# Three weight-splitting steps moved behind a pair's second addition, and one pair's x and convolution moved behind the gates, in a fused soft-cap attention and gated-convolution kernel

## The chip, the core and the metric

The kernel runs on one core of one Trainium2 chip. Such a core has four compute engines that run their own instruction streams in order and meet at semaphores: TensorE (PE, matmuls; its weight loads are shown as PEld), VectorE (DVE), ScalarE (ACT) and GpSimd (POOL); SyncE (SP) issues the DMAs here. The metric is the time of one execution in microseconds (us).

## The reference

Soft-capped attention over 8 batches, 12 heads, 448 positions and head size 64, then a gated causal convolution and two projections over 768 channels:

```
scores = cap * tanh(q @ k.T / sqrt(64) / cap)
attn   = softmax(scores);  x = attn @ v            # heads side by side: x is (8, 448, 768)
gate   = sigmoid(sum over k<5 of conv_w[k] * x shifted by k rows)
out    = (gate * (x @ w_val)) @ w_out              # weights are float64 in memory
```

## The kernel before

**Pairs.** Two heads make a pair, six pairs a batch, 48 pairs p in all (pair p belongs to batch p // 6). For each pair q and k are loaded in 32-column blocks and turned on DVE (L291); four key chunks i of 112 rows give scores on PE (`pss`, L312), tanh and exp on ACT (L320, L324, tile `pt`), the product with v on PE (`psa`, L349), and the row sums on PE (`psz`, L361). To save PE work DVE first adds exponentials of chunks: `add` i=0 for chunks 0 and 1, i=1 ("the second addition") for chunks 2 and 3 (both L334, tile `pa`), and from pair 11 on a third one that joins the two (L331). Pairs 7 to 10 feed both sums to PE, so that `psz` has one matmul couple on the first sum and one on the second. DVE then turns the sums (L369, `zt`), forms reciprocals (L375, L376), spreads them (L382) and multiplies (L390) into `u`, the transposed x of the pair.

**x and the convolution.** ACT rounds `u` to `xh` (L395), DVE takes the rest `xl` (L226), and the five taps build the pre-gate: the first on ACT (L407) up to pair 10 and on DVE (L409) from pair 11, the others on DVE (L411).

**Projections.** When a batch's six x are there, one `val` per 128 columns accumulates 18 matmuls in a `psf` bank (L432 to L434), ACT takes the sigmoids (L417), DVE multiplies (L438, "gate"), ACT rounds to `g_h` (L441), DVE takes the rest `g_l` (L226), and `out_part` multiplies with `wo` (L461 to L463) into a `psf` bank that ACT copies to `osb` (L469) for the store. There are two `psf` banks.

**Weights.** `w_val` and `w_out` are split into two float32 parts in twelve steps n = 0 to 11, called W0 to W11 here. A step has a `first` on ACT (L126, L127), a `second` on DVE (L130, L131) and a `third` on DVE (L134 to L136). W0 to W5 make `wv`, W6 to W8 the first half of the columns of `wo`, W9 to W11 the second half. Raw tiles are single: W n's raw load (L258) is issued when W n-1's `second` has read its tile.

**Order.** Nothing is scheduled automatically: each step gets a due time in units of pairs, from tables (`PAIRED` for pairs 7 to 10, `STEADY` for 11 and 12, `SPLIT` after) or lists, and the sorted list is the order on every engine. Pair p's second addition is due at p + 1.03, W n's `first` at `W_AT[n]`, its `second` 0.02 and its `third` 0.05 later. `LATE_X` puts a pair's `xl` at p + 1.76 and its taps at p + 1.78 to 1.89 in place of 1.58 and 1.60 to 1.70; the loop gives it to the first pair of a batch (p % 6 == 0). Gates of batch b with due times from 6b + 7.62 on are multiplied in the pairs after the batch's last.

Of the kernel before, what the change touches and what calls it, by code (L numbers as in the profile page):

```python
# [86 lines left out]
NEARLY, NPAIRED, NPLAIN = 6, 11, 13  # L87
# [6 lines left out]
OUT_LATE = (9.80, 10.36, 10.74, 11.74, 12.36, 12.60)  # L94
PART = 0.13
KEEP_AT = 10.2
W_AT = (0.70, 1.70, 2.70, 3.70, 4.70, 5.70, 7.1, 8.0, 8.9, 9.7, 10.4, 11.0)
W_LOAD = -0.5
W_SECOND, W_THIRD, W_THIRD_EARLY = 0.02, 0.05, 0.71
W_FREE = 11.3  # L100
# [87 lines left out]
def fast_path(tc, io, u2, q, k, v, w_val, conv_w, w_out, out, capt):  # L188
# [9 lines left out]
    NP = B * NPAIR  # L198
# [12 lines left out]
    with ExitStack() as ctx:  # L211
# [264 lines left out]
        cw_steps = []  # L476
        events = []
        tables = [EARLY if p < NEARLY else SIXTH if p == NEARLY else PAIRED if p < NPAIRED else STEADY if p < NPLAIN else SPLIT for p in range(NP)]
        for p in range(NPLAIN, NP):
            if p % NPAIR == 0:  # L480
                tables[p] = tables[p] | LATE_X

        def at(when, f, *a):
            events.append((when, len(events), f, a))
# [19 lines left out]
        for b in range(B):  # L504
# [15 lines left out]
            for m, y in enumerate(OUT_ODD if b % 2 else OUT_LATE if b == B - 2 else OUT_EVEN):  # L520
# [3 lines left out]
                at(t0 + y + 0.40, store_out, b, m)  # L524
        for n, t0 in enumerate(W_AT):
            third = [x + (W_THIRD if x > NEARLY else W_THIRD_EARLY) for x in W_AT]
            at(W_AT[n - 1] + W_SECOND if n else W_LOAD, weight_load, n)
            at(third[n - 1] if n else W_LOAD, late_load, n)
# [135 lines left out]
def kernel(tc, q, k, v, cap, w_val, conv_w, w_out, out):  # L664
    nc = tc.nc
    with tc.tile_pool(name="cap_pool", bufs=1) as pool, tc.tile_pool(name="io", bufs=2) as io:
        capt = pool.tile([P, 1], F32, name="capt")
        nc.sync.dma_start(capt, cap.rearrange("(o c) -> o c", o=1).partition_broadcast(P))

        pad = conv_w.shape[0] - 1  # L670
        u2 = [pool.tile([P, pad + q.shape[2]], F32, name=f"u{i}") for i in range(2)]
        for t, src in zip(u2, (q, k)):
            load_blocks(nc, t[:, pad:], src, 0)
        mag = pool.tile([1, 1], F32, name="mag")
        nc.vector.scalar_tensor_tensor(mag, capt[0:1], -1.0, capt[0:1], ALU.mult, ALU.max)
        small = pool.tile([1, 1], I32, name="small")
        nc.vector.tensor_scalar(small, mag, CAP_FAST, None, ALU.is_le)
        flag = nc.values_load(small, min_val=0, max_val=1)
        with tc.If(flag != 0) as cmp:
            fast_path(tc, io, u2, q, k, v, w_val, conv_w, w_out, out, capt)  # L680
        with cmp.Else():
            general_path(tc, q, k, v, w_val, conv_w, w_out, out, capt)
# [30 lines left out]
```

## Time and profile before

| | |
|---|---|
| median of three runs | 754.6 us (752.79 to 754.98) |
| the profiled execution | 752.42 us |
| its span, first to last instruction | 750.7 us |
| PE busy | 725.2 us, 97% of the span |
| DVE busy | 592.8 us, 79% |
| ACT busy | 538.1 us, 72% |
| mean granted TensorE clock | 0.997 |

The profiled execution lies 2.2 us below the median, and 1.7 us of it lie outside the span. Durations below are from this execution. The trace lists instructions by start time, with the length of one or of a merged run, and in square brackets how long the engine sat idle just before and which instruction ended that. Merged runs overlap the next instruction by the pipeline's depth: three matmuls of one line 0.2 us apart each show 0.36 us.

### The profile page before, as it was taken

The page shows a single profiled execution, that of the slowest core. Times are in us where ns is not written, and L with a number is a line of the kernel's source. Part 1 is how long each engine was busy: PE and PEld are TensorE (multiplying, and loading weights), DVE is VectorE, ACT ScalarE, POOL GpSimd, SP SyncE. Part 2 cuts the span into 40 slices and gives each one's busy share as a digit, 9 for nine tenths or more (in the row PEclk, how much of TensorE's full clock was granted, in tenths as well). Part 3 has the DMA queues.
Part 4 walks back from the last instruction along what each step waited for, and adds up shares of the span by engine and source line. Part 5 has one row for each costly group of instructions (what it writes and reads, how often), then busy time and mean ns, then how long its engine had stood idle before and what let it go on. Part 6 is the DMA issues. An engine that isn't in the chain of part 4 may idle for free.

```text
span 750.7 us, 10859 instructions
## 1 busy us (share of the span) xinstructions
PE 725.2 (97%) x3972; PEld 487.0 (65%) x3972; DVE 592.8 (79%) x972; ACT 538.1 (72%) x708; POOL 7.5 (1%) x16
## 2 busy tenths in 40 slices
PE   5999998999899999999999999999999999999997
PEld 2333654557667777577677767767766776675997
DVE  2799988888987689888898769988898778997410
ACT  4899967777777687777957678686976669775311
POOL 0000000000000000000000000000000000000000
PEclk9999999999999999999999999999999999999999
DMA  6998866754223332234232333223322333210001
GB/s 111 225 214 193 221 162 147 198 122 77 44 38 80 80 74 38 49 81 83 48 61 49 80 71 68 44 68 73 72 38 60 82 77 53 50 34 22 22 21 67
DMA packets 241820, 63.75 MB, mean 85 GB/s; under 512 B 228448, under 2 KB 235616, under 8 KB 241760
## 3 DMA queue, kind: packets, MB, share of 16 engines
q1 hardware_dynamic: 241760, 62.98, 38.0%
q8 instruction: 33, 0.54, 0.3%
q14 instruction: 27, 0.22, 0.1%
HBM read 51.94 MB, written 11.01 MB: 84 GB/s over the span
## 4 chain that ended last, share of the span: by engine, by line
PE 44%; DVE 24%; ACT 24%; issue 5%; SPq 2%; DMA 1%; DVEq 0%; ACTq 0%
ACT pt L320 7%; PE psf L461 7%; PE pss L312 7%; ACT pt L324 6%; PE psf L463 6%; PE psf L462 6%; PE psa L349 6%; DVE pa L334 5%; DVE gate L411 3%; ACT gate L417 3%; PE psf L432 3%; PE psz L361 2%; PE psf L434 2%; PE psf L433 2%; DVE g_l L226 2%
## 5 line engine op out<-in xcount | busy, mean ns | idle before, releaser
L320 ACT ACTIVATE pt<-pss,rc 112x896 f32<-112x896 f32 x192 | 185.8, 1004 | 29.0 <-PE pss L312 29.0
L324 ACT ACTIVATE pt<-pt,capt 112x896 f32<-112x896 f32 x192 | 189.3, 1039 | 0.1
L349 PE MATMUL psa<-pt,vn 112*64 112x448 f32 x720 | 147.7, 546 | 0.0
L411 DVE SCALAR_TENSOR_TENSOR gate<-u,cw,gate 128x448 f32<-128x448 f32 x192 | 132.4, 689 | 5.8
L461 PE MATMUL psf<-wo,g_h 128*128 128x384 f32 x336 | 116.9, 348 | 0.0
L463 PE MATMUL psf<-wo,g_l 128*128 128x384 f32 x336 | 112.7, 335 | 0.0
L462 PE MATMUL psf<-wo,g_h 128*128 128x384 f32 x336 | 112.5, 335 | 0.0
L432 PE MATMUL psf<-xh,wv 128*128 128x448 f32 x288 | 108.9, 378 | 2.1 <-DVE gate L438 2.0
L434 PE MATMUL psf<-xl,wv 128*128 128x448 f32 x288 | 104.4, 362 | 0.0
L433 PE MATMUL psf<-xh,wv 128*128 128x448 f32 x288 | 104.3, 362 | 0.0
L334 DVE TENSOR_TENSOR pa<-pt 112x896 f32<-112x896 f32 x84 | 91.1, 1084 | 12.6 <-ACT pt L324 12.6
L349 PEld LDWEIGHTS psa<-pt,vn 112*64 112x64 f32 x720 | 47.7, 136 | 81.2 <-issue 69.8
L395 ACT CAST xh<-u 128x448 fp32r<-128x448 f32 x48 | 27.1, 565 | 76.8 <-DVE u L390 76.7
L461 PEld LDWEIGHTS psf<-wo,g_h 128*128 128x128 f32 x336 | 63.0, 188 | 22.6 <-issue 18.3
L369 DVE STREAM_TRANSPOSE zt<-psz 128x448 f32<-128x448 f32 x45 | 28.9, 642 | 57.1 <-PE psz L361 57.0
L432 PEld LDWEIGHTS psf<-xh,wv 128*128 128x128 f32 x288 | 54.0, 187 | 28.0 <-issue 18.3
L441 ACT CAST g_h<-gate 128x448 fp32r<-128x448 f32 x48 | 26.3, 563 | 51.9 <-DVE gate L438 51.8
L463 PEld LDWEIGHTS psf<-wo,g_l 128*128 128x128 f32 x336 | 63.1, 188 | 0.3
L462 PEld LDWEIGHTS psf<-wo,g_h 128*128 128x128 f32 x336 | 63.1, 188 | 0.0
L312 PE MATMUL pss<-qt,kt 64*112 64x448 f32 x208 | 50.6, 606 | 9.6 <-DVE guard L235 7.8
L469 ACT COPY osb<-psf 128x384 f32<-128x384 f32 x56 | 26.8, 479 | 44.3 <-PE psf L463 44.3
L312 PE MATMUL pss<-qh,kh 64*112 64x448 f32 x280 | 58.5, 412 | 0.0
(74 smaller groups left out, 906.4 us busy)
## 6 DMA issues: line engine op xcount, KB each, us to landing
vn<-in_v_dram SPq DMA_DIRECT2D x96, 112.0 KB, 2.6
out_dram<-osb SPq DMA_DIRECT2D x56, 192.0 KB, 1.9
qn<-in_q_dram SPq DMA_DIRECT2D x188, 56.0 KB, 2.5
kn<-in_k_dram SPq DMA_DIRECT2D x188, 56.0 KB, 2.4
w_raw<-in_moe_w_val_dram SPq DMA_DIRECT2D x12, 384.0 KB, 4.5
w_late<-in_moe_w_val_dram SPq DMA_DIRECT2D x12, 384.0 KB, 4.3
w_raw<-in_moe_w_out_dram SPq DMA_DIRECT2D x12, 384.0 KB, 3.7
w_late<-in_moe_w_out_dram SPq DMA_DIRECT2D x12, 384.0 KB, 4.6
```

What stands on the lines that cost most here:

```text
L312: nc.tensor.matmul(ps[:CH, j, :S], st[x][r, c], st[y][r], start=(n == 0), stop=(n == len(parts) - 1))
L320: nc.scalar.activation(st["p", i], st.pop(("s", i)), AF.Tanh, scale=rc8[:CH])
L324: nc.scalar.activation(t, t, AF.Exp, scale=capt[:CH])
L334: nc.vector.tensor_tensor(st["a", i], st["p", 2 * i], st["p", 2 * i + 1], op=ALU.add)
L349: nc.tensor.matmul(st["o"][r, :S], vloads[p][:, j, i], t[:, j], start=(i == 0), stop=(i == NKT - 1))
L411: nc.vector.scalar_tensor_tensor(g, u[:, i:i + S], cw[:, hp, i:i + 1], g, ALU.mult, ALU.add)
L432: nc.tensor.matmul(o, w_h, xh, start=(c == 0), stop=False)
L433: nc.tensor.matmul(o, w_l, xh, start=False, stop=False)
L434: nc.tensor.matmul(o, w_h, xl, start=False, stop=(c == NCC - 1))
L461: nc.tensor.matmul(o, g_h[:, d, s], w_h, start=(d == 0), stop=False)
L462: nc.tensor.matmul(o, g_h[:, d, s], w_l, start=False, stop=False)
L463: nc.tensor.matmul(o, g_l[:, d, s], w_h, start=False, stop=(d == NCC - 1))
```

## The change

Three entries of `W_AT` are raised and the loop that gives out `LATE_X` starts at pair 11 in place of 13, which adds pair 12 (the first pair of the third batch, due when the second batch's gates are).

```diff
-W_AT = (0.70, 1.70, 2.70, 3.70, 4.70, 5.70, 7.1, 8.0, 8.9, 9.7, 10.4, 11.0)
+W_AT = (0.70, 1.70, 2.70, 3.70, 4.70, 5.70, 7.1, 8.035, 9.035, 9.7, 10.4, 11.035)
...
-        for p in range(NPLAIN, NP):
+        for p in range(NPAIRED, NP):
             if p % NPAIR == 0:
                 tables[p] = tables[p] | LATE_X
```

**W8 on DVE** (near 117 to 124 us of the trace). `pa_1086` before and `pa_1072` after are the same tile, the second addition of pair 8; the first five rows before are W8's. Before:

```order
L226 TENSOR_TENSOR g_l<-gate,g_h 128x448
L130 TENSOR_SCALAR w_t<-w_t 128x768
L131 TENSOR_TENSOR wo<-w_t,w_raw 128x2x384
L134 TENSOR_SCALAR w_late<-w_late 128x2x384
L135 TENSOR_SCALAR w_t<-wo 128x768
L136 SCALAR_TENSOR_TENSOR wo<-w_late,w_t 128x2x384
L438 TENSOR_TENSOR gate<-psf,gate 128x448
L334 TENSOR_TENSOR pa_1086<-pt 112x896
L226 TENSOR_TENSOR g_l<-gate,g_h 128x448
```

After, on the same engine at the same place:

```order
L226 TENSOR_TENSOR g_l<-gate,g_h 128x448
L438 TENSOR_TENSOR gate<-psf,gate 128x448
L334 TENSOR_TENSOR pa_1072<-pt 112x896
L226 TENSOR_TENSOR g_l<-gate,g_h 128x448
L130 TENSOR_SCALAR w_t<-w_t 128x768
L131 TENSOR_TENSOR wo<-w_t,w_raw 128x2x384
L134 TENSOR_SCALAR w_late<-w_late 128x2x384
L135 TENSOR_SCALAR w_t<-wo 128x768
L136 SCALAR_TENSOR_TENSOR wo<-w_late,w_t 128x2x384
```

All five W8 steps stand behind a gate product, the second addition and a `g_l`; on ACT, W8's L126 and L127 stand behind the rounding `g_h` (L441) of that gate in place of ahead of it. W7 and W11 move by less: only their L130 and L131 stood ahead of the second addition (of pairs 7 and 10), and stand right behind it now, with L134 to L136 as before; ACT's order does not change there.

**Pair 12 on DVE** (near 187 to 196 us). `u_63` is pair 12's x. Before, from the `kl` of the next pair on:

```order
L226 TENSOR_TENSOR kl<-kt,kh 128x448
L226 TENSOR_TENSOR xl<-u_63,xh 128x448
L409 TENSOR_SCALAR gate<-u_63,cw 128x448
L411 SCALAR_TENSOR_TENSOR gate<-u_63,cw,gate 128x448
L438 TENSOR_TENSOR gate<-psf,gate 128x448 x2
L411 SCALAR_TENSOR_TENSOR gate<-u_63,cw,gate 128x448 x3
L226 TENSOR_TENSOR g_l<-gate,g_h 128x448 x2
L438 TENSOR_TENSOR gate<-psf,gate 128x448
L334 TENSOR_TENSOR pa_1745<-pt 112x896
```

After:

```order
L226 TENSOR_TENSOR kl<-kt,kh 128x448
L438 TENSOR_TENSOR gate<-psf,gate 128x448 x2
L226 TENSOR_TENSOR g_l<-gate,g_h 128x448 x2
L226 TENSOR_TENSOR xl<-u_63,xh 128x448
L409 TENSOR_SCALAR gate<-u_63,cw 128x448
L411 SCALAR_TENSOR_TENSOR gate<-u_63,cw,gate 128x448 x4
L438 TENSOR_TENSOR gate<-psf,gate 128x448
L334 TENSOR_TENSOR pa_1745<-pt 112x896
```

Two gate products and their two `g_l` stand ahead of pair 12's six steps, which still stand ahead of the third gate product and the second addition of pair 13. The instructions of PE, POOL and SP stand in the same order in both kernels; a weight's raw load on SP still waits for the `second` of the weight before it.

## Rows read from the trace of the kernel before

**Rows 1.** The page's chain that ended last, shares of the span by engine.

```profile
PE 44%; DVE 24%; ACT 24%; issue 5%; SPq 2%; DMA 1%; DVEq 0%; ACTq 0%
```

**Rows 2.** Waits of PE, 80 to 220 us: total, times, longest.

```profile
PE psz L361 <- DVE pa L334: 4.1, 3, 2.3
```

**Rows 3.** Timeline around W7 (start, length, engine, line), 99 to 108 us.

```profile
100.40 1.96 ACT L324 ACTIVATE pt<-pt,capt 112x896 f32<-112x896 f32 x2
...
103.20 0.56 DVE L130 TENSOR_SCALAR w_t<-w_t 128x768 int32<-128x768 int32 x1 [1.11 <-ACT w_t L126]
...
105.05 1.09 DVE L334 TENSOR_TENSOR pa<-pt 112x896 f32<-112x896 f32 x1
...
106.06 0.58 DVE L134 TENSOR_SCALAR w_late<-w_late 128x768 int32<-128x768 int32 x1
...
106.19 0.97 PE L361 MATMUL psz<-pa,ones 112*64 112x448 f32 x4 [0.65 <-DVE pa L334]
```

**Rows 4.** Timelines of DVE, ACT and PE around W8, 116 to 144 us.

```profile
118.98 0.56 DVE L130 TENSOR_SCALAR w_t<-w_t 128x768 int32<-128x768 int32 x1 [1.65 <-ACT w_t L126]
119.95 0.96 DVE L131 TENSOR_TENSOR wo<-w_t,w_raw 128x768 fp32r<-128x768 f32 x1 [0.41 <-ACT w_raw L127]
...
125.91 0.61 DVE L369 STREAM_TRANSPOSE zt<-psz 128x448 f32<-128x448 f32 x1
...
123.41 0.56 ACT L441 CAST g_h<-gate 128x448 fp32r<-128x448 f32 x1 [3.50 <-DVE gate L438]
...
130.38 0.89 ACT L126 ACTIVATE w_t<-w_raw 128x768 f32<-128x768 f32 x1
...
132.10 1.00 ACT L320 ACTIVATE pt<-pss,rc 112x896 f32<-112x896 f32 x1
...
121.16 0.92 PE L361 MATMUL psz<-pa,ones 112*64 112x448 f32 x4
...
125.44 3.30 PE L312 MATMUL pss<-qt,kt 64*112 64x448 f32 x8
131.99 1.01 PE L312 MATMUL pss<-qt,kt 64*112 64x448 f32 x4
133.15 1.01 PE L312 MATMUL pss<-qt,kt 64*112 64x448 f32 x4 [0.15 <-ACT pt L320]
...
137.15 1.67 PE L361 MATMUL psz<-pa,ones 112*64 112x448 f32 x8
142.08 1.76 PE L312 MATMUL pss<-qt,kt 64*112 64x448 f32 x8
```

**Rows 5.** Window 125.20 to 128.50: busy us by engine, PEclk, DMA share, GB/s.

```profile
125.20:128.50 3.30, 3.30 (x10) 1.08 (x8) 3.16 (x8) 2.50 (x4) 0.56 (x2) 0.50 1.12 275
```

**Rows 6.** Timeline of PE around W11, 152 to 156 us.

```profile
152.12 0.92 PE L361 MATMUL psz<-pa,ones 112*64 112x448 f32 x4
...
155.05 0.44 PE L461 MATMUL psf<-wo,g_h 128*128 128x384 f32 x1
```

**Rows 7.** Timelines of PE, DVE and ACT around pair 12's steps, 187 to 199 us.

```profile
190.43 0.47 PE L432 MATMUL psf<-xh,wv 128*128 128x448 f32 x1 [1.99 <-DVE gate L438]
...
198.71 0.92 PE L361 MATMUL psz<-pa,ones 112*64 112x448 f32 x4
...
196.87 1.09 DVE L331 TENSOR_TENSOR pa<-pa,pa 112x896 f32<-112x896 f32 x1
...
188.01 1.00 ACT L320 ACTIVATE pt<-pss,rc 112x896 f32<-112x896 f32 x1
190.47 1.04 ACT L441 CAST g_h<-gate 128x448 fp32r<-128x448 f32 x2 [1.46 <-DVE gate L438]
```

**Rows 8.** Window 187.79 to 197.96, from `kl`'s end to L331's: as rows 5.

```profile
187.79:197.96 10.17, 8.18 (x50) 5.43 (x48) 8.66 (x15) 8.68 (x12) 0.00 (x0) 1.00 0.07 12
```

**Rows 9.** W9's raw load: its issue, and its group's KB and us to landing.

```profile
120.94 0.82 SPq L258 DMA_DIRECT2D w_raw<-in_moe_w_out_dram  x2
...
w_raw<-in_moe_w_out_dram SPq DMA_DIRECT2D x12, 384.0 KB, 3.7
```

## The prediction

> **What bounds the kernel now.** I read the page's engine shares first: PE is busy 97% of the span, so only what stands in front of PE can be worth anything. Then the page's chain: PE holds 44% of it, DVE and ACT 24% each [rows 1], so the end is set in turns, by PE in some stretches and by DVE and ACT in others, although both are less busy. Then the list of PE's waits from 80 to 220 us, where the change acts: three waits of `psz` for the second addition, 4.1 us together, the longest 2.3 [rows 2]. One wait of 1.99 us of a `val` for a gate product follows at 190 us [rows 7]. The timelines show the three waits at W7, W8 and W11, each with the addition behind weight steps on DVE [rows 3, 4, 6]. These four places are costed in order. The question at each is which engine stands next in the chain once PE's wait is gone, since a stretch moves forward only as far as its last engine.
>
> **W7.** DVE idles 1.11 us in front of L130, for ACT's L126. The addition's inputs are there at 100.40 + 1.96 = 102.36, before L130 starts at 103.20 [rows 3]. Put ahead, the addition runs from 102.4 to 103.5, inside that idle time; L130 follows at once, and L131 still waits for ACT as before. What stood behind the addition, from L134 on, moves from 106.06 to the addition's old place at 105.05: DVE gains 1.0 us [rows 3]. PE loses its wait of 0.65. All instructions are still there, so nothing else is paid.
>
> **W8.** Here all five steps go behind, with ACT's two. DVE idled 1.65 + 0.41 = 2.06 us in them, for ACT [rows 4]. Afterwards it has the gate product, the addition and a `g_l` to do while ACT runs L126 and L127. I count what is left as 0.3 us in which the addition waits for the exponentials and 0.15 us in which L131 waits for L127, so DVE gains 2.06 - 0.45 = 1.6 us, and `zt` at 125.91 comes 1.0 + 1.6 = 2.6 us earlier. ACT loses the 3.50 us of waiting for that gate [rows 4], but what it does next, rounding pair 9's x, hangs on `zt`, so it too gains 2.6.
>
> PE could gain more. `psz` in one piece takes 1.67 us, so the scores could follow at 121.16 + 1.67 = 122.83 in place of 125.44: 2.6 us. [...] With W7's 0.65, PE would be 4.8 us ahead at the scores of 131.99. They need both score banks back from ACT: the second half started at 133.15 after 0.15 us of waiting for the tanh that began at 132.10, with W9's L126 and L127 ahead of it on ACT since 130.38 [rows 4]. So the DVE and ACT chain takes over: **2.6 us stay, and PE hands 2.2 back in a new wait**, before and between the halves of those scores. I take 2.6; the ends are 1.0 (W7's part on DVE alone) and 4.8 (no new wait).
>
> **W11.** As W7: the addition fits the idle time in front of L130 and DVE gains 1.0. PE's `psz` in one piece would end at 152.12 + 1.67 = 153.79; `out_part` started at 155.05 [rows 6], so PE gains 1.3. Of the two PE is the later one in the next pair. I take 1.3, with 1.0 as the low end. W11 itself ends as much earlier as DVE runs earlier, and `out_part` needs it only at its fifth of six blocks, some 2 us in.
>
> **Pair 12.** The first gate product now follows `kl` at 187.8 and frees the `psf` bank 2 us sooner, so the `val` at 190.43 loses its 1.99 us [rows 7]. Behind it stand the second product, two `g_l` and pair 12's six steps, and then the second addition of pair 13 and L331, which ended at 196.87 + 1.09 = 197.96; `psz` at 198.71 needs that [rows 7]. The work on DVE up to there is the same; it idled 10.17 - 8.66 = 1.5 us in this window [rows 8]. The gate product no longer waits, but the `g_l` do: ACT starts the first rounding behind the tanh of 188.01 to 189.01 [rows 7], so DVE, done with both products at about 188.9, waits to 189.5, 0.6 us. L331 then ends at 197.96 - 1.5 + 0.6 = 197.1; PE would be at `psz` at 198.71 - 2.0 = 196.7. It waits 0.4 and **1.5 to 1.6 us stay; I take 1.5**, since `zt` behind it on DVE loses a little more. The ends are 2.0, and nothing if the waits for `g_h` add up to 2.2 us; beyond that it would lose. `xl` and the taps of pair 12 are wanted a batch later.
>
> **Queues.** SP's order is unchanged. W9's raw load waits for W8's L131, which now ends at about the same clock time as before less half a us, while its reader on ACT comes 2.6 us sooner. It was issued at 120.94 and read from 130.38 [rows 4, 9]: the 9.4 us between them shrink to about 7.3, against 3.7 us to landing [rows 9]. That cover holds; a later landing would cost ACT, one for one.
>
> **Sum.** 2.6 + 1.3 + 1.5 = 5.4 us. The profiled execution took 752.42, so it would take 747.0; against the median of 754.6 that is **749.2 us**. All of it is gone by 200 us; the rest is the same work.
>
> **Rivals.**
> (1) *The new wait lets the clock fall again.* PE now sits about 1 us, computes the first half of the scores, and sits over 1 us again. If the granted clock goes to half after that, the next scores, `psa` and `psz` pay what rows 4 show for one such spell, 1.5 us, and `zt` behind them is late by it: 3.9 us are saved, 750.7. [...] Against: there is work between them, and 1.99 us in one piece at 190 us leave a window at 1.00 [rows 7, 8]. [...]
> (2) *Pair 12's move gives nothing*, because the waits for `g_h` eat the idle time: 3.9 saved, 750.7.
> (3) *PE keeps all it could gain*, no new wait behind W8: 4.8 + 1.3 + 2.0 = 8.1 saved, 746.5. Against it stands the tanh of 132.10 behind W9's step.
> (4) *The additions are not done sooner for the chain.* If L130 to L136 come later by the whole 1.1 us of an addition each time, DVE's `zt` stays where it was at all three places, PE's gain goes back at the next scores, and pair 12's 1.5 are all: 753.1, no change by the bound below. Against it: in all three places DVE idles over 1 us for ACT in front of L130.
> (5) *Slower: W9's raw data come late.* ACT's L126 heads a queue with the tanh that PE waits for. If the load took over 7.3 us from its issue, every us more would be paid; at 7.3 + 5.4 = 12.7 us all gains are gone, and at 15 us the kernel takes 756.9. For it: the loads of q and k are issued sooner too, and the DMA engines are full there (share 1.12, rows 5). Against: 3.7 us as a median [rows 9].
> That the change does not do what it says is excluded by the order: the additions do stand ahead.
>
> **How the numbers follow.** My forecast has 0.52, rival 1 has 0.16, rival 2 0.10, rival 3 0.05, rival 4 0.12, rival 5 0.05. Runs of this kernel scatter by about 2 us, and 0.3% (2.3 us) is about what a measurement can tell from no change. The range takes in rivals 1, 2 and 3 and some scatter above the first two: 746.2 to 752.0; it leaves out rivals 4 and 5. Faster by over 0.3% (below 752.3) are the forecast and rivals 1 to 3: 0.83. Within 0.3%: rival 4, 0.12. Slower: rival 5, 0.05.
>
> **What would show it.** Right: no `psz` waits for L334 at W7, W8 and W11; `zt` behind W8 2.6 us earlier; new waits of PE for tanh just ahead of the scores that stood at 131.99 and 133.15, some 2 us in all; a granted clock of 1.00 where it was 0.50; the `val` of 190.43 without a wait and a new `psz` wait of about 0.4 us for L331. Wrong: a clock of 0.50 behind the new waits (rival 1), ACT idle in front of W9's L126 for a DMA (rival 5), or shifts of DVE's `zt` that stay at zero while PE's waits vanish (rival 4).

## The result, and the profile after

The changed kernel takes 750.33 us, the median of 12 runs (747.65 to 753.48), against 754.63 us for the kernel before beside it (12 runs, 752.58 to 757.06). The ratio is 0.9937, with a 95% interval from 0.9921 to 0.9952: faster by 4.3 us, and by 3.6 to 6.0 us over the interval. The forecast was 5.4 us faster, at 749.2. The profiled execution took 749.64 us with a span of 747.9, against 752.42 and 750.7 before.

The page's totals say little. The first line is the page's span, the second its engine shares; the third is the chain and answers to [rows 1].

```profile
span 747.9 us, 10860 instructions
PE 724.3 (97%) x3972; PEld 488.3 (65%) x3972; DVE 593.0 (79%) x972; ACT 537.7 (72%) x708; POOL 9.0 (1%) x16
PE 43%; DVE 25%; ACT 16%; issue 4%; SPq 1%; DMA 1%; DVEq 0%; ACTq 0%
```

PE's share stays at 97% and the chain is still set in turns. PE's waits from 80 to 220 us (total, times, longest) tell more; they answer to [rows 2]:

```profile
PE pss L312 <- ACT pt L320: 3.3, 3, 1.6
PE psz L361 <- DVE pa L331: 0.3, 1, 0.3
```

The three `psz` waits for L334, 4.1 us, are gone. In their place stand waits of the scores for the tanh, 3.3 us, of which the first kernel had 0.15 [rows 4], and 0.3 us for L331. So PE got back some 4 us and, at once, waited 3 us of it somewhere else.

**How the shift is counted.** At pair 6, ahead of everything that the change touches, the trace of after is already 0.70 us later than that of before. Some 0.6 us of that came where DVE waited for a DMA, which it did not in before:

```profile
90.97 0.57 DVE L134 TENSOR_SCALAR w_late<-w_late 128x768 int32<-128x768 int32 x1 [0.48 <-DMA w_late<-in_moe_w_out_dram]
```

That is not the change: over the executions profiled here the `zt` of pair 6 (L369 on DVE) starts anywhere from 93.24 to 96.22 us. In three of them (w11_only, p12_only and w9_later below) the granted clock was 0.50 from about 26 to 29 us, and pair 1's `zt` already starts 1.3 to 2.4 us later than in before; in the others it lies within 0.8 us of before. So I count from pair 6's `zt`. The table gives the start of a later pair's `zt` less that of pair 6, in before, and in the other kernels the difference to before.

| `zt` of pair | 7 | 8 | 9 | 10 | 11 | 12 | 13 | 14 | 46 | 47 |
|---|---|---|---|---|---|---|---|---|---|---|
| before, us | 15.81 | 32.11 | 45.07 | 63.23 | 75.32 | 89.46 | 105.88 | 120.24 | 588.49 | 599.10 |
| after | -0.98 | -2.19 | -2.20 | -3.23 | -3.56 | -3.55 | -4.54 | -5.01 | -5.07 | -5.08 |
| after_again | -0.97 | -2.18 | -2.19 | -3.19 | -3.53 | -3.53 | -4.51 | -5.00 | -5.06 | -5.07 |

The steps at pairs 7, 8, 10 to 11 and 13 to 14 are W7, W8, W11 and pair 12's move. From pair 14 on nothing more is gained: 5.1 us in all.

**W7 and W8 on DVE** in after (start, length, engine, line; in brackets the idle time before, and what ended it), answering to [rows 3, 4]:

```profile
103.10 1.09 DVE L334 TENSOR_TENSOR pa<-pt 112x896 f32<-112x896 f32 x1 [0.30 <-ACT pt L324]
104.11 0.55 DVE L130 TENSOR_SCALAR w_t<-w_t 128x768 int32<-128x768 int32 x1
104.89 0.97 DVE L131 TENSOR_TENSOR wo<-w_t,w_raw 128x768 fp32r<-128x768 f32 x1 [0.23 <-ACT w_raw L127]
...
117.89 1.09 DVE L334 TENSOR_TENSOR pa<-pt 112x896 f32<-112x896 f32 x1 [0.30 <-ACT pt L324]
118.90 0.62 DVE L226 TENSOR_TENSOR g_l<-gate,g_h 128x448 fp32r<-128x448 f32 x1
119.43 0.56 DVE L130 TENSOR_SCALAR w_t<-w_t 128x768 int32<-128x768 int32 x1
120.18 0.99 DVE L131 TENSOR_TENSOR wo<-w_t,w_raw 128x768 fp32r<-128x768 f32 x1 [0.19 <-ACT w_raw L127]
121.08 0.88 DVE L134 TENSOR_SCALAR w_late<-w_late 128x768 int32<-128x768 int32 x1
...
124.42 0.60 DVE L369 STREAM_TRANSPOSE zt<-psz 128x448 f32<-128x448 f32 x1
```

The 1.11, 1.65 and 0.41 us of DVE idling for ACT are down to waits of 0.2 to 0.3. One row had no counterpart in the prediction: L134 at W8 took 0.88 us in place of 0.56.

**The new wait.** PE behind W8, in after:

```profile
122.52 1.76 PE L312 MATMUL pss<-qt,kt 64*112 64x448 f32 x8
129.03 1.01 PE L312 MATMUL pss<-qt,kt 64*112 64x448 f32 x4 [1.42 <-ACT pt L320]
131.65 1.01 PE L312 MATMUL pss<-qt,kt 64*112 64x448 f32 x4 [1.61 <-ACT pt L320]
132.59 3.23 PE L349 MATMUL psa<-pt,vn 112*64 112x448 f32 x16
```

The first row took 3.30 us before [rows 4], at a granted clock of 0.50 [rows 5], right behind this wait of PE:

```profile
124.43 1.08 PE L361 MATMUL psz<-pa,ones 112*64 112x448 f32 x4 [2.35 <-DVE pa L334]
```

That wait is gone, and the scores take 1.76 us. Then both halves of the next scores wait, 3.03 us together, for ACT's tanh.

**Pair 12** in after, answering to [rows 7]:

```profile
186.70 1.16 DVE L226 TENSOR_TENSOR g_l<-gate,g_h 128x448 fp32r<-128x448 f32 x2 [0.63 <-ACT g_h L441]
...
194.36 0.97 PE L361 MATMUL psz<-pa,ones 112*64 112x448 f32 x4 [0.31 <-DVE pa L331]
```

The `val` in front of which PE sat 1.99 us starts at once; the two waits that take its place are 0.63 us on DVE and 0.31 on PE.

**The clock.** Windows of after and then of before (busy us of PE, PEld, DVE, ACT and POOL with counts, then the granted clock, DMA share, GB/s), around W8 and around the last pair's end:

```profile
128.00:132.80 4.80, 2.16 (x10) 0.74 (x12) 4.60 (x8) 4.77 (x7) 0.00 (x0) 1.00 0.67 109
132.80:137.00 4.20, 4.20 (x24) 1.44 (x20) 3.92 (x6) 4.20 (x6) 0.00 (x0) 1.00 0.73 233
...
689.40:692.70 3.30, 3.30 (x13) 3.30 (x12) 2.54 (x6) 0.56 (x1) 0.00 (x0) 0.53 0.00 0
```

```profile
693.00:696.40 3.40, 3.40 (x21) 3.40 (x21) 2.63 (x6) 0.72 (x2) 0.00 (x0) 1.00 0.02 5
```

Behind the new waits at W8 the clock stayed at 1.00. But behind the last pair's `psz` it stood at 0.53 from 689.4 to 692.7, and PE did 13 matmuls where before did 21 in about the same time. Both kernels have the same wait there, in after and then in before:

```profile
687.51 0.97 PE L361 MATMUL psz<-pa,ones 112*64 112x448 f32 x4 [1.72 <-DVE pa L331]
```

```profile
691.89 0.97 PE L361 MATMUL psz<-pa,ones 112*64 112x448 f32 x4 [1.72 <-DVE pa L331]
```

So the difference of the two profiled spans, 2.8 us, is 5.08 won by the order, less 0.70 of the later start, less 1.58 lost behind the last `psz`.

### The profile page after: what moved, and what is told of

Its sections match the earlier page's. It is cut to its first block, busy times and chain, and to the rows that moved or that the text cites. A ratio compares the mean times of both kernels' runs of the same rounds, so it can differ in the third digit from the quotient of the medians.

```text
span 747.9 us, 10860 instructions
## 1 busy us (share of the span) xinstructions
PE 724.3 (97%) x3972; PEld 488.3 (65%) x3972; DVE 593.0 (79%) x972; ACT 537.7 (72%) x708; POOL 9.0 (1%) x16
## 4 chain that ended last, share of the span: by engine, by line
PE 43%; DVE 25%; ACT 16%; issue 4%; SPq 1%; DMA 1%; DVEq 0%; ACTq 0%
PE psf L461 8%; PE pss L312 7%; PE psf L463 7%; PE psf L462 7%; PE psa L349 6%; DVE pa L334 5%; ACT pt L320 5%; ACT pt L324 4%; DVE gate L411 4%; PE psz L361 3%; ACT gate L417 2%; PE psf L432 2%; DVE g_l L226 2%; PE psf L433 2%; PE psf L434 2%
## 5 line engine op out<-in xcount | busy, mean ns | idle before, releaser
L334 DVE TENSOR_TENSOR pa<-pt 112x896 f32<-112x896 f32 x84 | 91.1, 1084 | 13.3 <-ACT pt L324 13.3
L395 ACT CAST xh<-u 128x448 fp32r<-128x448 f32 x48 | 27.1, 565 | 77.1 <-DVE u L390 77.0
L369 DVE STREAM_TRANSPOSE zt<-psz 128x448 f32<-128x448 f32 x45 | 28.9, 641 | 56.3 <-PE psz L361 56.3
L441 ACT CAST g_h<-gate 128x448 fp32r<-128x448 f32 x48 | 26.3, 562 | 47.4 <-DVE gate L438 47.3
```

Of the source, the lines that this page charges most:

```text
L334: nc.vector.tensor_tensor(st["a", i], st["p", 2 * i], st["p", 2 * i + 1], op=ALU.add)
```

## Experiments

My theory: the four moves give what the table shows, each by itself and without a share in the others; W8 gave less than forecast because GpSimd got in the way of L134; and a stretch at half the granted clock (0.50 in before [rows 5], 0.53 in after) comes or doesn't come behind waits that stay the same, which scatters the runs. Rivals: the moves help each other (W8's gain needs W7's); ACT alone set W8's gain; the low clock is a result of the new order.

### One part at a time

Four kernels, each the kernel before with one edit:

```diff
w7_only
-W_AT = (..., 7.1, 8.0, 8.9, 9.7, 10.4, 11.0)
+W_AT = (..., 7.1, 8.035, 8.9, 9.7, 10.4, 11.0)
w8_only
+W_AT = (..., 7.1, 8.0, 9.035, 9.7, 10.4, 11.0)
w11_only
+W_AT = (..., 7.1, 8.0, 8.9, 9.7, 10.4, 11.035)
p12_only
-        for p in range(NPLAIN, NP):
+        for p in range(NPAIRED, NP):
```

> The kernel before with only W7 moved behind pair 7's second addition. Shifts are read on DVE's zt (L369) of a pair, counted from zt of pair 6, which stands ahead of all changes (before: pair 7 at 15.81, pair 8 at 32.11, pair 14 at 120.24 us from it). Theory (the chain there runs over DVE and ACT): pair 7's zt 1.0 us earlier, and the 1.0 us stay to pair 14, although PE's wait was 0.65; W8's wait of PE stays at 2.3 us or a little more. Rival (the addition only pushes the weight step back by its own length): zt of pair 7 does not move, 0.0.

> The kernel before with only W8 moved. Theory: pair 8's zt 1.2 us earlier as in the changed kernel (1.6 were forecast; in the changed kernel L134 took 0.88 us in place of 0.56, beside GpSimd's copies of the gated tail, which the earlier rounding sets off), W8's wait of PE gone, a new wait of PE for tanh ahead of the next pair's scores of 2 to 3 us, and 1.2 us left at pair 14. Rival (PE sets the time): 2.4 us or more, 4 with the clock, left at pair 14, and no new wait.

> The kernel before with only W11 moved. Theory: DVE's zt of pair 10 1.0 us earlier, that of pair 11 1.3 us (PE is the later one there), 1.3 left at pair 14. Rival (the addition pushes W11 back, and the first output block of its half waits for it): less than 0.5 at pair 11 and a wait of PE's L461 for L136.

> The kernel before with only pair 12's xl and taps behind the gates. Theory: the val at 190.4 loses its wait of 1.99 us, a psz wait for L331 of 0.3 to 0.4 us appears, and 1.5 us are left at zt of pairs 13 and 14 (1.1 at pair 13, where DVE is late). Rival (the waits for g_h eat the idle time): 0.5 or less at pair 14. If the four parts are independent, the shifts of the four runs add up to the 5.0 us of the changed kernel.

One execution each: 753.93, 751.21, 756.58 and 755.38 us, the kernel before beside them 757.88. Shifts of `zt` as in the table above:

| `zt` of pair | 7 | 8 | 9 | 10 | 11 | 12 | 13 | 14 |
|---|---|---|---|---|---|---|---|---|
| w7_only | -0.96 | -0.93 | +0.72 | +0.53 | +0.53 | +0.53 | +0.53 | +0.53 |
| w8_only | -0.01 | -1.23 | -1.24 | -1.01 | -1.01 | -1.01 | -1.02 | -1.02 |
| w11_only | 0.00 | +0.01 | +1.63 | +0.43 | +0.10 | +0.10 | +1.70 | +1.69 |
| p12_only | 0.00 | 0.00 | +1.65 | +1.46 | +1.46 | +1.46 | +0.48 | +0.01 |

Each gain stands where its move is: 0.93 to 0.96 at W7; 1.22 at W8; 0.33 at pair 11 and 1.0 more than the others' 0.2 at pair 10 for W11, 1.34 together; 1.45 at pairs 13 and 14. The sum is 4.95, and the whole change has 5.01 there. W8's gain doesn't need W7's. But w8_only keeps only 1.02 at pair 14, where 1.2 was expected: the wait of `psz` in front of W11 is 1.34 us there in place of 1.11, and W11's move takes it away. These two moves share 0.2 us; of another share the table shows none.

What I had not expected is the +1.65 at pair 9 in the three kernels that leave W8 as it was. PE and the clock in w7_only:

```profile
124.28 0.97 PE L361 MATMUL psz<-pa,ones 112*64 112x448 f32 x4 [2.38 <-DVE pa L334]
125.18 1.76 PE L312 MATMUL pss<-qt,kt 64*112 64x448 f32 x8
130.37 1.01 PE L312 MATMUL pss<-qt,kt 64*112 64x448 f32 x4
133.00 1.67 PE L312 MATMUL pss<-qt,kt 64*112 64x448 f32 x4 [1.62 <-ACT pt L320]
134.60 3.84 PE L349 MATMUL psa<-pt,vn 112*64 112x448 f32 x14
```

```profile
133.40:136.70 3.30, 3.30 (x10) 0.77 (x8) 3.27 (x5) 3.30 (x5) 0.00 (x0) 0.51 0.47 131
```

In before the clock fell right behind the long `psz` wait, and the slow scores there cost nothing, since the next scores had to wait for ACT anyway [rows 4, 5]. Here it fell one step later, behind the 1.62 us wait of the scores, and `psa` and `psz` behind it were on the path: 1.65 us. The orders of before, w11_only and p12_only are the same up to there, and the low stretch began at 125.2 in the first [rows 5] and near 135 in the other two (0.50 from 136 to 138), behind the later wait. The price of a stretch at half the clock thus depends on where it begins: nothing in before, where PE has slack, 1.65 in w7_only, where PE sets the pace. In w11_only a second one, at 193 to 197 (0.50 from 194 on), took another 1.6 (pair 13), behind the same wait of 1.99 us for a gate that left the clock at 1.00 in before [rows 7, 8]; in p12_only one stood at 694 to 698, behind the last `psz`.

### The changed kernel again, and GpSimd left out

> The changed kernel once more. Theory: the order's gain (5.0 us at zt of pair 14, counted from zt of pair 6) comes back to 0.1 us, while the spells of half clock fall elsewhere or not at all: in the first execution one fell behind the 1.72 us wait ahead of the last psz, for 1.6 us, and none behind the new wait at W8; each such spell is 1.5 to 1.7 us of the time. Rival (the half clock belongs to a place): again one spell, behind the last psz, and none elsewhere.

749.72 us, beside 754.38 of before on that chip. The shifts (first table) repeat to 0.04 us, as expected. But the clock was low at the same place again, behind the last `psz` from 689 to 692 (0.50), and nowhere else from pair 1 up to there: this is what the rival said, and in no_keep0 (below) it happened once more (0.50 from 688 to 690). In w8_only and w9_later, with the same 1.72 us wait, it did not.

For L134, GpSimd's queue in after and then in before:

```profile
118.39 1.96 POOL L448 TENSOR_SCALAR g_h<-g_h 128x384 fp32r<-128x384 f32 x1 [101.58 <-ACT g_h L441]
120.33 1.22 POOL L448 TENSOR_SCALAR g_l<-g_l 128x384 fp32r<-128x384 f32 x1
```

```profile
124.06 1.22 POOL L448 TENSOR_SCALAR g_h<-g_h 128x384 fp32r<-128x384 f32 x1 [107.33 <-ACT g_h L441]
125.25 0.51 POOL L448 TENSOR_SCALAR g_l<-g_l 128x384 fp32r<-128x384 f32 x1
```

The rounding of the gate (L441) now comes ahead of W8's steps on ACT and sets GpSimd off, 5.7 us sooner, on copies that keep the batch's tail (`keep_tail`). L134 ended at 121.96, L135 began at 121.88, and the second copy ended at 121.55. The experiment leaves this copy out for the first batch; a second edit, not shown, writes zeros into the tail at the start in its place, so that batch 1's first output rows lack it:

```diff
-            if b % 2 == 0:
+            if b % 2 == 0 and b:
                 at(t0 + KEEP_AT, keep_tail)
```

> The changed kernel without GpSimd's copy of the first batch's gated tail (batch 1's first output rows then lack it; a write of zeros at the start takes its place). Theory (W8 gave 1.2 in place of 1.6 us because GpSimd's copies hold up DVE's L134): L134 at W8 takes 0.56 us in place of 0.88, and zt of pair 8 stands 29.5 to 29.6 us behind zt of pair 6 in place of 29.92. Rival (the shortfall is in the waits that I counted): 29.9 and L134 still at 0.88.

```profile
119.80 0.56 DVE L134 TENSOR_SCALAR w_late<-w_late 128x768 int32<-128x768 int32 x1
```

The kernel takes 747.93 us, and L134 is back at 0.56. Pair 8's `zt`, 29.58 us behind pair 6's, stands at -2.53 in place of -2.19 and pair 14's at -5.38 in place of -5.01: 0.35 us that stay. So it was GpSimd's copy that held L134, and not ACT.

### W9 moved as well

The same move for W9, behind its pair's L334:

```diff
-W_AT = (..., 8.035, 9.035, 9.7, 10.4, 11.035)
+W_AT = (..., 8.035, 9.035, 9.76, 10.4, 11.035)
```

> The changed kernel with W9's first due 0.06 later, so that on ACT both tanh stand ahead of it. Theory (behind W8 the DVE and ACT chain sets the pace, PE's new waits of 1.42 and 1.61 us are slack): the second of the two waits goes, PE starts psz of pair 9 up to 1 us sooner, but zt of pair 9 gains only the 0.6 us that DVE idled in front of it; 0.6 to 0.7 left at pair 11. Rival (PE's waits are lost time): 1.5 us or more at zt of pair 9 and pair 11.

A miss, at 749.82 us. Pair 9 won the 0.65 us (-2.85), but pair 10 stood at -3.19 and pair 11 at -3.49, as without the move. The DVE of w9_later in pair 10:

```profile
138.67 0.24 DVE L376 RECIPROCAL rc<-rc 128x14 f32<-128x14 f32 x1
139.33 0.56 DVE L130 TENSOR_SCALAR w_t<-w_t 128x768 int32<-128x768 int32 x1 [0.42 <-ACT w_t L126]
140.28 0.96 DVE L131 TENSOR_TENSOR wo<-w_t,w_raw 128x768 fp32r<-128x768 f32 x1 [0.39 <-ACT w_raw L127]
141.16 0.64 DVE L382 STREAM_TRANSPOSE zt<-rc 128x448 f32<-128x448 f32 x1
...
143.62 0.61 DVE L390 TENSOR_TENSOR u<-psa,zt 128x448 f32<-128x448 f32 x1
```

W10's L130 and L131 stand between the reciprocal (L376) and its spreading (L382) and wait for ACT, and ACT in turn waits 4.02 us for L390's `u` before it can go on to the tanh (up to L395 at 144.27 in the same kernel), for which the scores at 146.73 wait 0.69 us. `u` comes 4.95 us behind the reciprocal, against 4.26 in after_again: what pair 9 gave, pair 10 took.

### Two versions that go on from there

tail_paired gives the last pair the times that pairs 11 and 12 have for additions and sums, so that its `psz` needs L334 and not L331:

```diff
+        tables[NP - 1] = tables[NP - 1] | {"add": (0.52, 1.03), "sums": (1.28, 1.29)}
```

> The changed kernel with the last pair's two sums given to PE one by one (two more matmuls, no L331), so that PE waits 0.6 us in place of 1.72 ahead of the last psz. Theory: 1.1 us less from zt of pair 46 to the end of the last pair's psz, and no spell of half clock behind it, so about 1.6 us less than an execution that has one. Rival (any wait there brings the spell): the granted clock falls there in this run too.

One execution, 748.43 us (before 754.38). The last pair won 1.18 us more than pair 46 (shifts of -3.64 and -4.82), the 1.72 us wait is gone and the clock at the end is 1.00. But the shift at pair 9 is -0.57 in place of -2.20: this time the clock fell at the new waits behind W8. PE and the window in tail_paired:

```profile
128.68 1.01 PE L312 MATMUL pss<-qt,kt 64*112 64x448 f32 x4 [1.46 <-ACT pt L320]
131.31 1.84 PE L312 MATMUL pss<-qt,kt 64*112 64x448 f32 x4 [1.61 <-ACT pt L320]
133.08 3.99 PE L349 MATMUL psa<-pt,vn 112*64 112x448 f32 x16
```

```profile
131.40:134.70 3.30, 3.30 (x10) 0.97 (x12) 3.25 (x5) 3.30 (x5) 0.00 (x0) 0.51 0.38 106
```

Up to 131 us the kernel does exactly what after does. After_again had the same two waits, 1.46 and 1.61, and kept 1.00; this execution did not. That is the prediction's rival 1, at its price of 1.6, in one execution and not in the other.

> The kernel of tail_paired again, timed. [...] Rival: the stretch at W8 comes in most executions once the one at the tail is gone, and the time is that of the changed kernel, 750.

Timed, it takes 748.14 us (6 runs, 745.71 to 749.59) against 753.81 of before (11 runs, 752.18 to 756.35): 0.992, interval 0.9896 to 0.9945. Its profile shows the low stretch at W8 again (0.62 over 131.4 to 135.3, pair 9 at -0.56), and once more 1.18 at the last pair. So both profiled executions have that stretch, as the rival said, yet the time is not its 750. It is the 0.992 that I had estimated from tail_paired's profile (6.2 us of order gain, out of 754.4); two of the six runs, at a mean clock of 1.000 and 0.999, took only 745.71 and 746.00.

The last kernel has tail_paired's edit and W9's, and moves W10 behind L390 and its pair's first addition:

```diff
-W_AT = (..., 8.035, 9.035, 9.7, 10.4, 11.035)
+W_AT = (..., 8.035, 9.035, 9.76, 10.5, 11.035)
```

> The changed kernel with three more moves. The second additions and sums of the last pair come at the places that the pairs 11 and 12 have (tail_paired showed 1.18 us of order gain there). W9 moves behind its pair's third step (9.7 to 9.76; w9_later showed 0.65 us at pair 9, given back by pair 10). New: W10's five DVE steps move behind pair 10's normalizing product (L390) and first addition (10.4 to 10.5), so that 3.7 us of them no longer stand between pair 10's recip and its u, for which ACT waits 4.02 us (xh<-u, L395) in after_again. [...] Rival: ACT's own work (W9's and W10's exponents and roots, about 1.8 us each) sets the pace there and the scores still wait about 0.7 us: pair 10 stays at 3.2, pair 47 at 6.2.

**746.03 us** (6 runs, 745.59 to 747.57) against the same 753.81: 0.9898, interval 0.9878 to 0.9917. It is the fastest of the kernels here. DVE and ACT in pair 10:

```profile
138.69 0.24 DVE L376 RECIPROCAL rc<-rc 128x14 f32<-128x14 f32 x1
138.96 0.65 DVE L382 STREAM_TRANSPOSE zt<-rc 128x448 f32<-128x448 f32 x1
139.64 0.62 DVE L390 TENSOR_TENSOR u<-psa,zt 128x448 f32<-128x448 f32 x1
...
140.30 0.57 ACT L395 CAST xh<-u 128x448 fp32r<-128x448 f32 x1
```

`u` comes 0.95 us behind the reciprocal in place of 4.95, ACT no longer waits for it, and the 0.69 us wait of the scores is gone: what w9_later gave back had been lost to that chain, as I had expected. The size was not as expected: -2.80 at pair 10, -3.87 at 11, -5.31 at 14, -6.48 at 47, where I had estimated -3.85, -5.65 and -6.9 for pairs 10, 14 and 47 (after_again's shifts, the 0.65 us of w9_later, and at pair 47 the 1.18 of tail_paired). The next in the row was a DMA:

```profile
150.04 0.92 ACT L126 ACTIVATE w_t<-w_raw 128x768 f32<-128x768 f32 x1 [3.47 <-DMA w_raw<-in_moe_w_out_dram]
```

W11's raw load is issued on SP at 144.03, 48.60 us behind pair 6's `zt` and so no later than in after_again (48.67), but ACT is now there sooner and waits for it, and DVE's `zt` of pair 10 stands behind W11's steps. ACT's L126 started 6.0 us behind the start of that issue; in before the median from issue to landing was 3.7 [rows 9]. Of the 0.65 us some 0.3 are left (pairs 11 and 14). This is the mechanism of the prediction's rival 5, two weights later, and it cost half of what W9's and W10's moves were to bring.

So the order of the last kernel is only 0.2 to 0.3 us ahead of tail_paired's, while its median is 2.1 us lower. All its six runs have a mean clock of 0.999 or 1.000, those of tail_paired 0.994 to 1.000. Most of the 2.1 us is thus probably the clock: W9's move leaves one wait of 1.45 us where tail_paired has two, of 1.46 and 1.61. That it is the reason was not tested by itself.

## Why the prediction was right, and where it was off

**What bounds, and where the gain goes: right.** The question put at each place, which engine is next once PE's wait is gone, had the right answer at all four: DVE at W7, the chain of DVE and ACT at W8, PE at W11, L331 in pair 12.

**W7: right.** 1.0 forecast, 0.98 measured.

**W8: right in kind, one term too large.** 1.6 forecast, 1.21 measured. The waits that were to be left on DVE, 0.45, are 0.30 + 0.19. The step that failed is "DVE gains 2.06 - 0.45": it took every step's own length as fixed. L134 took 0.32 us more, because the rounding that was put ahead of W8 on ACT sets off GpSimd's `keep_tail`; no_keep0 gives 0.35 back. The prediction's part on queues looked at SP's order, and never asked what else L441 releases. The hand-back of PE was forecast as 2.2 and is 3.0 (2.7 in no_keep0), ahead of and between the halves of the scores, as said. It cost no more than forecast, since it lies beside the chain that sets the pace. PE's 4.8 us in the prediction are 2.6 and 0.65, and 1.5 for the slow scores, which took 3.30 us at a granted clock of 0.50 [rows 4, 5]; in after they took 1.76.

**W11: right**, 1.3 forecast and 1.36 measured, first as 1.0 on DVE at pair 10 and then as 0.3 more of PE at pair 11.

**Pair 12: right**, 1.5 forecast and 1.46 measured; `g_l` waits 0.63 (0.6 forecast), `psz` 0.31 (0.4).

**W9's load (rival 5): did not come.** ACT's L126 of W9 started at 128.88 with no wait for a DMA.

**Sum.** 5.4 forecast, 5.0 to 5.1 measured in the order; the missing 0.4 is GpSimd.

**The clock: rival 1 was real, and at the wrong place.** Behind the new waits the clock fell in two of the six executions profiled with both of them (tail_paired twice; not in after, after_again, w8_only and no_keep0), at a price of 1.6, so the forecast that it stays at 1.00 held in most. What the prediction didn't see is the 1.72 us wait of the last `psz`, unchanged by the edit, behind which the clock fell in four of nine executions profiled with it: after, after_again, no_keep0 and p12_only, not before, w7_only, w8_only, w11_only and w9_later. It fell in three of the four executions that have the whole change, and in one of the five that have a part of it or none; so few don't settle whether the new order has a share in this place. Over whole runs it shows none: the mean clock is 0.996 in the 12 runs of the changed kernel (0.993 to 1.000) and 0.996 in the 11 of the kernel before beside tail_paired (0.990 to 0.999). "All of it is gone by 200 us; the rest is the same work" was true of the order and not of the time.

Of the 1.1 us between 749.2 and 750.33 the order explains 0.4. The rest, 0.7, is less than this measurement can tell: the interval, 3.6 to 6.0 us saved, holds the order's 5.0 as well as the forecast's 5.4. Stretches of 1.6 us and the 3 us over which pair 6's `zt` scatters can well make up 0.7; that they do is argued and not shown, since only one of the 12 executions has a trace. The median alone would not have told the forecast from its rivals either: 750.33 lies nearer to the 750.7 of rivals 1 and 2. What speaks for the forecast is the trace: pair 12's 1.46 us against rival 2, and the clock of 1.00 behind W8, in that execution, against rival 1.

What makes the clock fall no run here shows: 1.46 and 1.61 us of waiting came with a fall in tail_paired (0.51), and the same two without one in after_again (1.00).

## What to carry to other kernels

When a wait of the busiest engine is taken away, follow the chain to the engine that comes next, and to whatever the moved instruction releases: an earlier rounding set off a copy on GpSimd that slowed a step on DVE. To compare two traces, count from an instruction ahead of the change; a start that was 0.7 us later would otherwise have hidden a part of the gain. A wait of PE that seems to cost little can have a stretch at half the clock behind it in some executions and not in others (the 1.72 us wait of the last `psz` in four of nine), so one profile doesn't show its price.

## What the runs showed of the hardware

Of the stretches at half the granted clock that the windows show, those at 689.4 to 692.7 in after (0.53), 133.4 to 136.7 in w7_only (0.51) and 131.4 to 134.7 in tail_paired (0.51) cost about 1.6 us each (1.58, 1.65 and 1.63), where PE set the pace. The one at 125.2 to 128.5 in before (0.50 [rows 5]) cost nothing, since the work behind it had to wait for another engine.

GpSimd's two copies and one step of DVE were slower beside each other. `keep_tail`'s two copies took 3.2 us together in after (118.39 to 121.55), where DVE ran L226, L130, L131 and L134 beside them, and 1.7 in before (124.06 to 125.76), beside L334, L226 and L291; L134 took 0.88 us in place of 0.56. For L134 no_keep0 shows the cause: 0.56 us with the copies gone. For the copies it is not tested. L134 ended at 121.96, 0.41 us behind the end of the second copy. Two other steps of DVE, L226 and L130, started behind the first copy and kept their 0.62 and 0.56 us.
